# Sums of the input for the seven-product phase: formed in the normalisation phase and the ramp instead of in the attention's units

## The chip, the cores and the metric

One core of one Trainium2 chip. The metric is the device time in microseconds (us) of one execution, as the median of several runs.

## The reference

A transformer block on 2048 tokens of width 640, all in float32. Attention and a gated feed-forward network work on the same normalised input and are both added to it:

```python
xn = layernorm(x)                                # over the last axis, no weights
q, k, v = split(xn @ wqkv)                       # 32 heads of 20
mask = (i - j >= 0) & (i - j < 256)              # sliding causal window
o = softmax(where(mask, q @ k.T / sqrt(20), -1e9)) @ v
a = o @ wo
h = gelu(xn @ w_gate, approximate=True) * (xn @ w_up)     # 1728 wide
return x + a + h @ w_down
```

## The kernel before

The tokens are four chunks of 512, and the normalised input is kept transposed on chip, for each chunk as a high part `xh0` to `xh3` and a low part `xl0` to `xl3` (128 partitions, five blocks of the width, 512 tokens). Float32 products are made of three products of such parts.

**Normalisation.** For each chunk c the kernel loads and normalises four tiles of 128 tokens, transposes them on TensorE (`ln_turn`, ps_t), splits them into high and low, and makes v of the chunk before (`proj_v`, ps_v) and the first 128 columns of q and of k (`proj_qk`, ps_d). `save_qk` splits each of these into three bfloat16 parts; the last step of it is a subtraction on GpSimd (POOL, L259), and SyncE (SP, L268) then stores it to DRAM as `qd` or `kd`. POOL also makes the masks there (L467 to L473). In this part the instructions are placed by a scheduler.

**Ramp and units.** The attention is cut into 32 units: eight groups of four heads times four chunks. The order in it is written out by hand, in slots: fourteen for each unit, and ahead of unit 0 a ramp of twelve steps that are numbered -13 to -2. In the ramp `load_stack` brings q and k of the first units from DRAM into `qs` and `ks` (L494; six loads each, three for either half of the heads), and `max_pair` makes the first row maxima (ps_m on PE, L523). A unit makes the exponentials (ps_e, L582, and P on ACT, L584), POOL sets the masked corners of P to zero (`clear`, L595 and L598), and `av_unit` multiplies them with v (ps_o, L622). Between these, `pull_fill` puts in other matmuls: further columns of q, k and v, and part of the feed-forward network.

Each engine takes its instructions in the order in which they were written. SP has one queue: loads and stores alike are issued in turn, and one whose data isn't ready holds those behind it.

**The sums.** After the attention, columns of the feed-forward network are made with seven products instead of eight. That needs four sums of blocks of the input for each pair p of chunks. `x_sums(p, k, half)` forms them: ten steps s1 to s10 on POOL (L755), each a `tensor_tensor` on 128 partitions and 256 tokens, and each on the result of the one before it in its sum. Four of the steps (s3, s5, s7, s10) end a sum, which SP then stores to DRAM in `td` (L759). There are eight such calls (two pairs, two values of k, two halves), so 80 steps and 32 stores. A sum lies in one of two buffers, so a third sum waits until the first has been stored. Before, the steps are put into the units:

```python
XS0, XSN = 24, 50
for i, (p, k, half) in enumerate((p, k, half) for p in range(NC // 2) for k in range(2) for half in range(2)):
    for j, fn in enumerate(x_sums(p, k, half)):
        at(XS0 + XSN * i + 2 * j, when_free, fn)
```

`at` sets the slot, `when_free` puts the step into a waiting list, and `release(2)` takes two of that list in certain slots of a unit. `defer(n, ...)` does something n slots later, or at once where no slots run, as in the normalisation.

Of the kernel before, what the change touches and what calls it, by code (L numbers as in the profile page):

```python
# [9 lines left out]
F32 = mybir.dt.float32  # L10
# [3 lines left out]
OP = mybir.AluOpType  # L14
# [5 lines left out]
C = 512  # L20
NC = S // C
# [23 lines left out]
NQD = 9  # L45
OWN = 4, 5
WARM = 64
XS0, XSN = 24, 50
RAMP = 4.0
GAP = 16  # L50
VW = 1408
# [19 lines left out]
def block_kernel(ctx, tc, x, wqk, wv, wgu, wdo, wdl, out):  # L71
    nc = tc.nc
# [123 lines left out]
    def at(slot, fn, *a):  # L196
        acts.setdefault(slot, []).append((fn, a))
# [23 lines left out]
    def flush():  # L221
        while lates:
            fn, a = lates.pop(0)
            fn(*a)
# [4 lines left out]
    def defer(n, fn, *a):  # L229
        if now[0] is None:  # L230
            fn(*a)
        else:
            at(now[0] + n, fn, *a)

    def load_qk(t):
        raw = wrp.tile([128, KT, 128], F32, name="wr", tag="wr")
        nc.sync.dma_start(raw, wqk[t])
        return raw
# [106 lines left out]
    def first_chunk(xs, wr0, wr5, lp):  # L345
# [74 lines left out]
                save_qk(5 * i, 0, dn[i])  # L420
        return w0, w5, mv

    v0 = []
    with tc.tile_pool(name="lp", bufs=1, side="right") as lp:
        xs = [ln_load(t, lp) for t in range(2)]
        wr0 = load_qk(0)
        xs += [ln_load(t, lp) for t in range(2, 4)]
        warm = lp.tile([128, 256], BF, name="warm")[:, 0:128]
        nc.vector.memset(warm, 0.0)
        ps = psd.tile([128, C], F32, name="ps_u", tag="dn")  # L430
        for i in range(WARM):
            nc.tensor.matmul(ps[:, 0:128], warm, warm, start=True, stop=True)
        wr5 = load_qk(5)
        prep = load_v(0, v0, lp)
        next(prep)
        xs += [ln_load(t, lp) for t in range(4, 8)]
        w0, w5, mv1 = first_chunk(xs, wr0, wr5, lp)
        run(prep)
        v0 = v0[0]
        ones = lp.tile([4, 2 * C], BF, name="ones")  # L440
        nc.gpsimd.memset(ones, 0.0)
        nc.gpsimd.memset(ones[0:2], 1.0)
        for i in range(NK):
            for j in (0, 2):
                nc.sync.dma_start(ks[i][SR:64, j:j + 2].rearrange("p j t -> p (j t)"), ones)
        for c in range(1, NC):
            ln_scale(xs[4 * c:4 * c + 4], lp, mv1 if c == 1 else None)
            vs = [proj_v(v0, 4 * c - 4 + i, None if i % 2 else (psm, "mx")) for i in range(4)]
            if c == 1:
                with tc.manual_schedule(engines={mybir.EngineType.PE}):  # L450
                    lead = (cost for gen in vs for cost in gen)
                    for _ in range(VLEAD):
                        next(lead)
                    ln_turn(4 * c, xs[4 * c:4 * c + 4])
                    run(lead)
            else:
                ln_turn(4 * c, xs[4 * c:4 * c + 4])
            if c + 1 < NC:
                xs += [ln_load(t, lp) for t in range(4 * c + 4, 4 * c + 8)]
            if c == 1:  # L460
                for i in range(NQ):
                    for j in (0, 2):
                        nc.sync.dma_start(qs[i][SR + 2:64, j:j + 2].rearrange("p j t -> p (j t)"), ones[2:4])
            if c == 2:
                for z in range(4):
                    band = mask if z == 0 else lp.tile([128, D], F32, name="xi", tag="xi", bufs=8)[:, 0:288]
                    nc.gpsimd.memset(band, 0.0)  # L467
                    nc.gpsimd.affine_select(out=band, in_=band, pattern=[[1, 288]], compare_op=OP.is_ge,
                                            fill=NEG, base=32 * z - 1, channel_multiplier=-1)
                    nc.gpsimd.affine_select(out=band, in_=band, pattern=[[-1, 288]], compare_op=OP.is_ge,  # L470
                                            fill=NEG, base=256 - 32 * z, channel_multiplier=1)
                    if z:
                        nc.gpsimd.tensor_copy(mask[32 * z:32 * z + 32], band[32 * z:32 * z + 32])  # L473
                raws1 = [load_qk(1), load_qk(6)]
            if c < NC - 1:
                run(*vs)
                run(proj_qk(0, w0, c), proj_qk(5, w5, c))
            else:
                run(*[proj_v(v0, 4 * c - 4 + i) for i in range(VEARLY)])
# [261 lines left out]
            ws = nxt  # L741
        rest.append(ws)

    def x_sums(p, k, half):
        w = C // 2
        a, b = (slice((2 * p + i) * C + half * w, (2 * p + i) * C + half * w + w) for i in (0, 1))
        eh, el = xh.bitcast(F32), xl.bitcast(F32)
        live = {}

        def tile_of(i):  # L750
            live[i] = ap.tile([128, w], F32, name="tx", tag="tx")
            return live[i]

        def pool(o, i, j, op):
            nc.gpsimd.tensor_tensor(out=o, in0=i, in1=j, op=op)  # L755

        def store(i):
            t = live[i]
            defer(4, lambda: nc.sync.dma_start(td[p][i][:, k, half * w:half * w + w], t))  # L759

        def s1():
            pool(tile_of(1), eh[:, k, b], eh[:, k, a], OP.subtract)

        def s2():
            pool(live[1], live[1], el[:, k, b], OP.add)

        def s3():
            pool(live[1], live[1], el[:, k, a], OP.subtract)
            store(1)

        def s4():
            pool(tile_of(2), eh[:, k + 2, b], live[1], OP.subtract)

        def s5():
            pool(live[2], live[2], el[:, k + 2, b], OP.add)
            store(2)

        def s6():
            pool(tile_of(4), eh[:, k + 2, a], live[2], OP.subtract)

        def s7():
            pool(live[4], live[4], el[:, k + 2, a], OP.add)
            store(4)

        def s8():
            pool(tile_of(3), eh[:, k + 2, b], eh[:, k, b], OP.subtract)

        def s9():
            pool(live[3], live[3], el[:, k + 2, b], OP.add)

        def s10():
            pool(live[3], live[3], el[:, k, b], OP.subtract)
            store(3)

        return s1, s2, s3, s4, s5, s6, s7, s8, s9, s10

    NU = NG * NC
    stream = ((u, i) for u in range(NU) for i in range(8))
    fill = filler()
# [15 lines left out]
    def pull_fill(n):  # L815
        debt[0] += n
        while debt[0] > 0:
            debt[0] -= next(fill, 1.0)

    def attention():  # L820
        now[0] = -1
        load_stack(0)
        load_stack(1)
        load_stack(2)
        for i, (p, k, half) in enumerate((p, k, half) for p in range(NC // 2) for k in range(2) for half in range(2)):
            for j, fn in enumerate(x_sums(p, k, half)):
                at(XS0 + XSN * i + 2 * j, when_free, fn)
        for i in range(12):
            now[0] = i - 13
            for fn, a in tick():  # L830
                fn(*a)
            if i % 2 == 0:
                pull_max(2, now[0])
            flush()
            pull_fill(2 * RAMP)
        pull_fill(GAP / 2)
        pull_max(2, now[0])
        pull_fill(GAP / 2)
        for u in range(NU + 1):
            for i in range(NS):  # L840
                T = now[0] = NS * u + i
                for fn, a in tick():
                    fn(*a)
                if i in BURSTS:
                    pull_max(2, T)
                if i == 0 and u:
                    av_unit(u - 1)
                    flush()
                    pull_max(2, T)
                for s in SCORES.get(i, ()) if u < NU else ():  # L850
                    exp_piece(u, s)
                flush()
                if i in POOL_SLOTS or T < NS:
                    release(2)
                if u + 3 < NU and i in (KSLOT, 12):
                    load_stack(u + 3, (int(i == KSLOT),))
                pull_fill(RATE / NS)
        while acts or idle:
            now[0] += 1
            for fn, a in tick():  # L860
                fn(*a)
            flush()
            release(2)
        assert not idle
        now[0] = None
        run(fill)
        assert not acts
# [207 lines left out]
    class Job:  # L1075
# [24 lines left out]
        def store(self):  # L1100
            if self.kind == "r":
                nc.sync.dma_start(rd[self.i].rearrange("h (a t) -> (h a) t", a=4), self.t)
            elif self.kind == "t":
                nc.sync.dma_start(wtd[self.i], self.t)
            else:
                nc.sync.dma_start(self.rows, self.t)
# [417 lines left out]
```

## Time and profile before

| | us |
|---|---|
| median of 3 runs | 1049.04 |
| lowest and highest of them | 1048.1, 1049.57 |
| the profiled execution's own time | 1047.65 |
| its span in the profile | 1045.9 |

All rows of the profile are from that one execution. PE is TensorE's matmuls, PEld its weight loads, DVE VectorE, ACT ScalarE, POOL GpSimd, SPq the issues of SyncE's DMA queue. A row of a timeline has the start and the length in us, the engine, the line, the operation, what it writes and reads, and how many such instructions in a row it stands for; in brackets stands how long the engine was idle before it and what ended that. The granted clock is the share of full speed that TensorE had.

### The profile page before, as it was taken

How to read it: one execution, taken by the hardware profiler on the slowest of the kernel's cores; microseconds unless marked ns; L12 is line 12 of the kernel's file. 1: busy time of each engine (PE TensorE's matmuls, PEld its weight loads, DVE VectorE, ACT ScalarE, POOL GpSimd, SP SyncE). 2: the span in 40 equal slices, each digit the busy share in tenths (PEclk: the TensorE clock that was granted, in tenths of full speed). 3: DMA queues.
4: the chain of work that ended last, by engine and by line, in shares of the span. 5: the costliest groups of instructions: out<-in, count | busy, mean ns of one | idle time of the engine just before them, and what ended most of it. 6: DMA issues, size and time to landing. Idle time of an engine off the chain costs nothing.

```text
span 1045.9 us, 28723 instructions
## 1 busy us (share of the span) xinstructions
PE 1028.8 (98%) x10941; PEld 853.0 (82%) x10941; DVE 726.2 (69%) x2007; ACT 527.7 (50%) x1120; POOL 378.1 (36%) x543
## 2 busy tenths in 40 slices
PE   8999999999999999999999999999999999999998
PEld 7987767667788876767677888888888999999998
DVE  8845656666665565666663678877655889888887
ACT  4444667766666666656666532223324554333332
POOL 5222878876575567574745111110110000000000
PEclk9999999999999999999999999999999999999999
DMA  5641465545332354444322557676216874443342
GB/s 200 189 150 60 143 192 148 181 143 181 108 114 81 97 170 120 140 125 147 103 88 69 196 191 237 222 252 247 99 62 248 269 240 137 136 127 116 122 137 92
DMA packets 105203, 158.95 MB, mean 152 GB/s; under 512 B 15420, under 2 KB 60092, under 8 KB 105064
## 3 DMA queue, kind: packets, MB, share of 16 engines
q1 hardware_dynamic: 102680, 150.95, 45.1%
q10 hardware_dynamic: 2384, 6.16, 1.9%
q8 instruction: 86, 1.41, 0.5%
q14 instruction: 53, 0.43, 0.1%
HBM read 101.78 MB, written 54.92 MB: 150 GB/s over the span
## 4 chain that ended last, share of the span: by engine, by line
PE 87%; DVE 4%; DMA 3%; POOL 2%; SPq 1%; issue 1%; ACT 1%; DVEq 0%; POOLq 0%; ACTq 0%
PE ps_g L968 21%; PE ps L1235 21%; PE ps_d L110 20%; PE ps_e L582 7%; PE ps_v L110 7%; PE ps_o L622 5%; PE ps_m L523 4%; DVE junk L527 1%; PE ps_g L110 1%; DMA qs<-qd 1%; DMA ks<-kd 1%; PE ps_t L181 1%; SPq L494 1%; POOL pt L259 1%; PE ps_d L356 1%
## 5 line engine op out<-in xcount | busy, mean ns | idle before, releaser
L527 DVE CUSTOM_DVE_ANT_0 junk<-ps_m,mask 128x288 bf16<-128x288 f32 (+2 forms) x512 | 227.8, 445 | 143.0 <-PE ps_m L523 85.2
L584 ACT ACTIVATE P<-ps_e 128x512 f32<-128x512 f32 (+2 forms) x384 | 195.4, 573 | 59.4 <-PE ps_e L582 57.9
L1235 PE MATMUL ps<-wb,at 128*128 128x320 f32 x999 | 156.1, 309 | 0.1
L1235 PEld LDWEIGHTS ps<-wb,at 128*128 128x128 f32 x999 | 148.9, 188 | 0.5 <-issue 0.3
L595 POOL TENSOR_SCALAR_AFFINE_SELECT P<-P 128x512 f32<-128x512 f32 x128 | 84.2, 660 | 83.0 <-ACT P L584 75.4
L582 PE MATMUL ps_e<-qs,ks 124*128 124x128 bf16 (+2 forms) x704 | 107.1, 277 | 1.3 <-DVE mx L527 1.2
L110 PE MATMUL ps_d<-xh,wqh 128*128 128x512 f32 x350 | 105.2, 410 | 0.0
L110 PE MATMUL ps_d<-xh,wql 128*128 128x512 f32 x350 | 105.2, 410 | 0.0
L110 PE MATMUL ps_d<-xl,wqh 128*128 128x512 f32 x350 | 105.2, 409 | 0.0
L1235 PE MATMUL ps<-wt,at 128*128 128x320 f32 x552 | 89.3, 309 | 0.4 <-DVE u L1073 0.4
L622 PE MATMUL ps_o<-P,v 64*32 64x320 f32 (+5 forms) x2816 | 84.4, 353 | 3.0 <-DVE mx L527 1.6
L582 PEld LDWEIGHTS <-ks 124*128 124x128 bf16 x704 | 51.6, 98 | 39.7 <-issue 22.8
L1235 PEld LDWEIGHTS ps<-wt,at 128*128 128x128 f32 x552 | 82.9, 188 | 0.9 <-DVE u L1073 0.9
L1189 ACT ACTIVATE at<-ss 128x512 fp32r<-128x512 f32 x59 | 37.3, 632 | 89.6 <-DVE ss L1073 89.6
L103 POOL TENSOR_TENSOR wql<-wr,wqh 128x640 fp32r<-128x640 f32 x11 | 17.7, 1610 | 173.9 <-PE ps_g L968 129.3
L598 POOL TENSOR_SCALAR_AFFINE_SELECT P<-P 128x512 f32<-128x512 f32 x112 | 71.5, 648 | 20.6 <-ACT P L584 20.4
L622 PEld LDWEIGHTS ps_o<-P,v 64*32 64x32 f32 x2816 | 66.6, 107 | 15.0 <-DVE mx L527 6.1
L110 PEld LDWEIGHTS ps_d<-xh,wql 128*128 128x128 f32 x350 | 63.9, 189 | 13.1 <-issue 1.9
L110 PEld LDWEIGHTS ps_d<-xl,wqh 128*128 128x128 f32 x350 | 63.6, 189 | 12.2 <-issue 1.7
L110 PEld LDWEIGHTS ps_d<-xh,wqh 128*128 128x128 f32 x350 | 63.2, 189 | 12.6 <-issue 0.9
L523 PE MATMUL ps_m<-ks,qs 60*32 60x96 bf16 (+5 forms) x3008 | 64.6, 244 | 4.1 <-DVE mx L527 2.0
L259 POOL TENSOR_TENSOR pt<-r,pt 128x512 bf16<-128x512 f32 x40 | 46.8, 1170 | 54.6 <-ACT pt L258 54.5
(196 smaller groups left out, 1887.0 us busy)
## 6 DMA issues: line engine op xcount, KB each, us to landing
hr<-hd SPq DMA_DIRECT2D x104, 128.0 KB
hd<-he SPq DMA_DIRECT2D x50, 256.0 KB
wr<-wgu SPq DMA_DIRECT2D x27, 320.0 KB
qs<-qd SPq DMA_DIRECT2D x64, 120.0 KB
ks<-kd SPq DMA_DIRECT2D x64, 120.0 KB
xi<-x SPq DMA_DIRECT2D x16, 320.0 KB
qs<-qd SPq DMA_DIRECT2D x64, 80.0 KB
ks<-kd SPq DMA_DIRECT2D x64, 80.0 KB
```

The source lines that it names most:

```text
L110: nc.tensor.matmul(ps, a(k), b(k), start=n == 0, stop=n == 3 * nk - 1)
L259: nc.gpsimd.tensor_tensor(out=pt[:, l, :], in0=r, in1=pt[:, 1, :], op=OP.subtract)
L523: nc.tensor.matmul(ps[32 * h:32 * h + 32, lo:hi], q[rows, j, q0:q0 + 32], keys, start=True, stop=True, tile_position=(64 * r, 32 * h))
L527: nc.vector.tensor_tensor_reduce(out=junk[:, 0:n], in0=ps[:, 0:n], in1=mask[:, 288 - n:288], scale=1.0, scalar=NEG, op0=OP.add, op1=OP.max ...
L582: nc.tensor.matmul(ps[:, col:col + n], k[0:QROWS, j, kc:kc + 128], q[0:QROWS, j, q0:q0 + n], start=True, stop=True)
L584: nc.scalar.activation(pt[:, j, lo:hi], ps[:, lo:hi], AF.Exp, scale=SCALE)
L595: nc.gpsimd.affine_select(out=a, in_=a, pattern=[[0, 4], [1, 128]], compare_op=OP.is_ge, fill=0.0, base=0, channel_multiplier=-1)
L598: nc.gpsimd.affine_select(out=a, in_=a, pattern=[[0, 4], [-1, 128]], compare_op=OP.is_ge, fill=0.0, base=-1, channel_multiplier=1)
L622: nc.tensor.matmul(halves[h][32 * j:32 * j + 32, q0:q0 + n], v[rows, w0_:w0_ + 32], pts[u, bi][rows, j, col:col + n], start=i == 0, stop=i ...
L968: nc.tensor.matmul(ps, i, j, start=first and n == 0, stop=n == len(work) - 1, skip_group_check=True)
L1189: nc.scalar.activation(hi[:, 3:7], s, AF.Copy)
L1235: nc.tensor.matmul(ps[bank][:, 0:HD], *work[bank][j], start=bank not in begun, stop=final[p, bank] == n and j == len(work[bank]) - 1, skip ...
```

## The change

The sums of the first pair are formed in the normalisation: behind the transposes of chunk 2 those with k = 0, behind chunk 3 those with k = 1. The sums of the second pair go into the ramp, from its step -10 on, two steps a slot, and `release(2)` is called in the ramp too. The stores come one slot after their sum instead of four; in the normalisation they come at once. There the sums lie in the two buffers `he`, which the attention uses later for the feed-forward network. `x_sums` itself moves up in the file.

```diff
-XS0, XSN = 24, 50
+XS0, XSN = -10, 6
...
         def tile_of(i):
-            live[i] = ap.tile([128, w], F32, name="tx", tag="tx")
+            live[i] = (ap.tile([128, w], F32, name="tx", tag="tx") if p else
+                       hp.tile([128, C], F32, name="he", tag="he", bufs=2)[:, 0:w])
             return live[i]
...
         def store(i):
             t = live[i]
-            defer(4, lambda: nc.sync.dma_start(td[p][i][:, k, half * w:half * w + w], t))
+            defer(1, lambda: nc.sync.dma_start(td[p][i][:, k, half * w:half * w + w], t))
...
                 raws1 = [load_qk(1), load_qk(6)]
+            if c > 1:
+                for half in range(2):
+                    for fn in x_sums(0, c - 2, half):
+                        fn()
             if c < NC - 1:
                 run(*vs)
...
-        for i, (p, k, half) in enumerate((p, k, half) for p in range(NC // 2) for k in range(2) for half in range(2)):
-            for j, fn in enumerate(x_sums(p, k, half)):
-                at(XS0 + XSN * i + 2 * j, when_free, fn)
+        for i, (k, half) in enumerate((k, half) for k in range(2) for half in range(2)):
+            for j, fn in enumerate(x_sums(1, k, half)):
+                at(XS0 + XSN * i + j // 2, when_free, fn)
...
             flush()
+            release(2)
             pull_fill(2 * RAMP)
```

The steps of the sums have L435 in the changed kernel, their stores L439, the loads of `load_stack` L552, the clears L653 and L656. Two places of the order follow.

SP, before, at the loads of unit 0: the second three loads of its keys (`ks0`) stand right behind the first three, and ahead of the first store of q of chunk 2 (`qd2`). Numbers are those of the buffers.

```order
L494 DMA ks0_169<-kd0_88 40x1024
L494 DMA ks0_169<-kd0_88 20x1024
L494 DMA ks0_169<-kd0_88 60x1024
L494 DMA qs1_167<-qd1_85 40x1024
L268 DMA qd2_86<-pt_902 80x3x512
```

SP, after, the same three loads with what stands between them and the first three:

```order
L439 DMA td04_103<-he_833 128x256
L268 DMA qd2_86<-pt_938 80x3x512
L439 DMA td03_102<-he_837 128x256
L268 DMA qd2_86<-pt_938 48x3x512
L439 DMA td01_100<-he_1035 128x256
L268 DMA kd2_90<-pt_962 80x3x512
L268 DMA kd2_90<-pt_962 48x3x512
L439 DMA td02_101<-he_1040 128x256
L439 DMA td04_103<-he_1044 128x256
L552 DMA ks0_169<-kd0_88 40x1024
L552 DMA ks0_169<-kd0_88 20x1024
L552 DMA ks0_169<-kd0_88 60x1024
```

The five stores of sums here are the end of the second call of `x_sums` and most of the third; six more stand further up, among the loads of `qs0` and of the first half of `ks0`.

POOL, before, ahead of and at the clears of unit 0's P:

```order
L259 TENSOR_TENSOR pt_1392<-r_1393,pt_1392 128x512
L595 AFFINE_SELECT P_1585<-P_1585 128x4x128
L598 AFFINE_SELECT P_1585<-P_1585 128x4x128
L595 AFFINE_SELECT P_1652<-P_1652 128x4x128
L259 TENSOR_TENSOR pt_1714<-r_1715,pt_1714 128x512
L595 AFFINE_SELECT P_1707<-P_1707 128x4x128
L598 AFFINE_SELECT P_1707<-P_1707 128x4x128
```

POOL, after, the second and the third of these three pieces of P:

```order
L653 AFFINE_SELECT P_1767<-P_1767 128x4x128
L435 TENSOR_TENSOR tx_1838<-tx_1838,xl2_82 128x256
L435 TENSOR_TENSOR tx_1851<-xh3_79,tx_1838 128x256
L259 TENSOR_TENSOR pt_1843<-r_1844,pt_1843 128x512
L435 TENSOR_TENSOR tx_1851<-tx_1851,xl3_83 128x256
L435 TENSOR_TENSOR tx_1877<-xh2_78,tx_1851 128x256
L653 AFFINE_SELECT P_1833<-P_1833 128x4x128
L656 AFFINE_SELECT P_1833<-P_1833 128x4x128
```

The steps tx_1838 to tx_1877 are of the last call; all earlier calls and most of this one stand ahead of the last clears. Before, no step of a sum stands ahead of them.

More of the change, by code (lines that the diff above doesn't have):

```diff
@@ L421, in first_chunk, with x_sums, tile_of, pool @@
         return w0, w5, mv
+    def x_sums(p, k, half):
+        w = C // 2
+        a, b = (slice((2 * p + i) * C + half * w, (2 * p + i) * C + half * w + w) for i in (0, 1))
+        eh, el = xh.bitcast(F32), xl.bitcast(F32)
+        live = {}
+        def tile_of(i):
+            live[i] = (ap.tile([128, w], F32, name="tx", tag="tx") if p else
+                       hp.tile([128, C], F32, name="he", tag="he", bufs=2)[:, 0:w])
+            return live[i]
+        def pool(o, i, j, op):
+            nc.gpsimd.tensor_tensor(out=o, in0=i, in1=j, op=op)
+        def store(i):
+            t = live[i]
+            defer(1, lambda: nc.sync.dma_start(td[p][i][:, k, half * w:half * w + w], t))
+        def s1():
+            pool(tile_of(1), eh[:, k, b], eh[:, k, a], OP.subtract)
+        def s2():
+            pool(live[1], live[1], el[:, k, b], OP.add)
+        def s3():
+            pool(live[1], live[1], el[:, k, a], OP.subtract)
+            store(1)
+        def s4():
+            pool(tile_of(2), eh[:, k + 2, b], live[1], OP.subtract)
+        def s5():
+            pool(live[2], live[2], el[:, k + 2, b], OP.add)
+            store(2)
+        def s6():
+            pool(tile_of(4), eh[:, k + 2, a], live[2], OP.subtract)
+        def s7():
+            pool(live[4], live[4], el[:, k + 2, a], OP.add)
+            store(4)
+        def s8():
+            pool(tile_of(3), eh[:, k + 2, b], eh[:, k, b], OP.subtract)
+        def s9():
+            pool(live[3], live[3], el[:, k + 2, b], OP.add)
+        def s10():
+            pool(live[3], live[3], el[:, k, b], OP.subtract)
+            store(3)
+        return s1, s2, s3, s4, s5, s6, s7, s8, s9, s10
     v0 = []
@@ L742, in filler @@
         rest.append(ws)
[L744 to L750, printed above, removed]
-            live[i] = ap.tile([128, w], F32, name="tx", tag="tx")
[L752 to L795, printed above, removed]
     NU = NG * NC
```

## The prediction

> **What bounds the kernel now.** I read the engine totals first.
>
> ```profile
> span 1045.9 us, 28723 instructions
> PE 1028.8 (98%) x10941; PEld 853.0 (82%) x10941; DVE 726.2 (69%) x2007; ACT 527.7 (50%) x1120; POOL 378.1 (36%) x543
> ```
>
> TensorE (PE) has 17.1 us of idle time in the whole span. So the change can give back only PE waits, and costs whatever new PE waits it makes. The busy time by stretch says where both can be (columns: stretch, length, busy time of PE, weight load, DVE, ACT, POOL, granted clock, DMA share, GB/s).
>
> ```profile
> 46.25:106.02 59.77, 58.78 (x576) 47.72 (x574) 28.81 (x103) 25.15 (x76) 14.34 (x16) 1.00 0.37 110
> 121.00:520.00 399.00, 391.88 (x6463) 288.09 (x6448) 253.35 (x968) 258.73 (x570) 278.75 (x411) 1.00 0.46 138
> ```
>
> In the first row, the end of the normalisation and the ramp, PE idles 0.99 us and POOL works 14.34 us of 59.77. In the second, the units in which the sums run, PE idles 7.12 us and POOL works 70% of the time. Moving work from the second row to the first looks free by share. The share hides two in-order queues, POOL and SP, so I read their timelines next.
>
> ```profile
> 43.61 2.27 SPq L494 DMA_DIRECT2D qs<-qd  x6
> 45.92 3.12 SPq L494 DMA_DIRECT2D ks<-kd  x6
> 49.08 0.33 SPq L494 DMA_DIRECT2D qs<-qd  x1
> 56.05 0.82 SPq L268 DMA_DIRECT2D qd<-pt  x2
> 61.80 2.81 SPq L494 DMA_DIRECT2D ks<-kd  x6
> 64.65 2.57 SPq L494 DMA_DIRECT2D qs<-qd  x6
> 67.27 2.56 SPq L494 DMA_DIRECT2D ks<-kd  x6
> 62.48 0.38 PE L523 MATMUL ps_m<-ks,qs 60*32 60x32 bf16 x28
> SPq L268 <- POOL pt L259: 77.8, 23, 13.4
> ```
>
> SP issues the loads of unit 0 (six of qs, six of ks) by 49.04, then stands until 56.05 at a store of q that POOL has not finished: an SP store holds everything behind it (77.8 us in 23 such waits, last row). The loads are 13.4 us ahead of the first score matmul on PE at 62.48. That lead is the cover of anything put ahead of them.
>
> **The change part by part.** First what a step of the sums costs.
>
> ```profile
> L755 POOL TENSOR_TENSOR tx<-tx,xl x48: 722/736/1274, 122.3 to 516.3; 128x256 f32<-128x256 f32 x48
> 121.44 0.73 POOL L755 TENSOR_TENSOR tx<-xh,xh 128x256 f32<-128x256 f32 x1
> 122.25 1.55 POOL L755 TENSOR_TENSOR tx<-tx,xl 128x256 f32<-128x256 f32 x2
> 24.52 1.33 POOL L259 TENSOR_TENSOR pt<-r,pt 128x512 bf16<-128x512 f32 x1 [1.69 <-ACT pt L258]
> 37.69 1.16 POOL L259 TENSOR_TENSOR pt<-r,pt 128x512 bf16<-128x512 f32 x1 [11.85 <-ACT pt L258]
> 45.81 0.44 POOL L473 COPY mask<-xi 32x288 f32<-32x288 f32 x1
> 69.83 3.10 POOL L103 TENSOR_TENSOR wql<-wr,wqh 128x640 fp32r<-128x640 f32 x2
> ```
>
> A step waits for the one before it, so it starts 0.80 us after it (121.44 to 122.25). The first five steps fall into the idle 11.85 us ahead of 37.69 and cost nothing; the others start when the masks end, at 45.81 + 0.44 = 46.25.
>
> Then the stores. Sums alternate between two buffers, so s6 of each half cannot start before the store issued after s3 has landed. Two landings that POOL waited for, with their issues:
>
> ```profile
> 395.17 2.41 SPq L759 DMA_DIRECT2D td<-tx  x2
> 398.56 0.74 POOL L755 TENSOR_TENSOR tx<-xh,tx 128x256 f32<-128x256 f32 x1 [2.33 <-DMA td<-tx]
> 291.47 3.84 SPq L759 DMA_DIRECT2D td<-tx  x3
> 293.41 0.74 POOL L755 TENSOR_TENSOR tx<-xh,tx 128x256 f32<-128x256 f32 x1 [0.86 <-DMA td<-tx]
> POOL tx L755: 7.2, 5
> ```
>
> Issue to use was 3.39 us and 1.94 us; of 32 stores 5 made POOL wait (last row: the us and times that POOL waited for td). Since only late ones leave a row I take 2.4, nearer the short end. Two steps (s4, s5; 1.6 us) cover part, so each half costs POOL about 0.85 us, and 0.3 to 1.8 us with the two ends.
>
> *The first stall.* The order puts eleven stores, which need 27 steps, ahead of the second three ks loads of unit 0. Five steps are early; 22 x 0.80 = 17.6 us, two L259 between them 2.3 us (1.16 each), two store waits 1.7 us: 46.25 + 21.6 = 67.9. SP issues that store and three loads, 0.4 us each, the last at 69.1. For load to use:
>
> ```profile
> 406.17 2.97 SPq L494 DMA_DIRECT2D qs<-qd  x6
> 411.27 0.45 PE L523 MATMUL ps_m<-ks,qs 60*32 60x32 bf16 x31 [0.63 <-DMA qs<-qd]
> ```
>
> The last of these six was issued at about 408.7 and PE had it at 411.27, so 2.6 us. PE starts its first pair at 71.7, not 62.48: 9.2 us of new wait, since the 13.4 us of lead are used up.
>
> *The end of the ramp.* POOL also clears the masked parts of P, which the first ps_o needs.
>
> ```profile
> 104.97 2.49 PE L622 MATMUL ps_o<-P,v 64*32 64x320 f32 x61
> 105.38 0.64 POOL L598 TENSOR_SCALAR_AFFINE_SELECT P<-P 128x512 f32<-128x512 f32 x1
> 105.97 0.64 POOL L595 TENSOR_SCALAR_AFFINE_SELECT P<-P 128x512 f32<-128x512 f32 x1
> ```
>
> The clear of 105.38 ends at 106.02, inside PE's ps_o group: no cover. The order puts 76 steps ahead of it, 71 of them after 46.25: 71 x 0.80 = 56.8 us, beside the 14.34 us that POOL works there already. Without a single wait the clear ends at 46.25 + 56.8 + 14.34 = 117.4, 11.4 us later than before. Store waits: six halves at 0.85 = 5.1 us. The first half of the second pair pays more: its first store stands behind 18 loads (ks1, qs2, ks2: 61.80 to 69.83 above, 8.0 us) and two stores of q (0.8 us), and lands 2.4 us later, 11.2 us after the last step of the first pair; POOL has five steps, two L259 and the two wql to do meanwhile (4.0 + 2.3 + 3.1 = 9.4 us), so it waits 1.8 us. So 117.4 + 6.9 = 124.3, and PE is 18.3 us late. The first stall lies inside this and is not added.
>
> *After it.* The waits that the sums caused in the units go:
>
> ```profile
> 403.44 3.42 PE L622 MATMUL ps_o<-P,v 64*32 64x384 f32 x55 [1.61 <-DVE mx L527]
> 402.23 1.23 POOL L595 TENSOR_SCALAR_AFFINE_SELECT P<-P 128x512 f32<-128x512 f32 x2
> 465.92 1.42 PE L622 MATMUL ps_o<-P,v 64*32 64x320 f32 x48 [1.27 <-POOL P L598]
> 401.50:403.40 1.90, 0.33 (x2) 0.00 (x0) 1.06 (x3) 0.36 (x1) 1.90 (x3) 1.00 0.08 23
> 403.40:406.80 3.40, 3.37 (x68) 2.56 (x75) 1.40 (x6) 0.27 (x1) 3.32 (x6) 0.52 0.77 217
> ```
>
> The wait of 1.61 us is named after DVE, but ends with POOL's clear (402.23 + 1.23), which was late by the 2.33 us that POOL stood at a td store above. Behind it the granted clock was 0.52 for 3.40 us, so 1.63 us more. With 1.27 at 465.92 and 0.63 at 411.27 the gain is 5.1 us; at most it is all 7.12 idle plus 1.63. What is late next there is PE's own work.
>
> The long waits of the ramp bring the same half clock: those inside the ramp are covered by POOL's delay, the last adds 1.6 us. [...]
>
> The sum: 18.3 + 1.6 - 5.1 = 14.8 us. The profiled execution took 1047.65, 1.75 us around its span, and becomes 1062.4; the median of the runs, 1049.04, is 1.39 us above it, so I forecast 1063.8. Nothing else is added or removed: PE, DVE and ACT have the same instructions in the same sequence in both orders.
>
> Bounds: with no store wait at all 11.4 - 5.1 = 6.3 us, 1055. With stores at 3.4 us each half costs 1.8 us, 13 us for seven and 1 for the hold-up: 117.4 + 14 = 131.4, 25.4 us late; two half clocks 3.2, less 2 to 5 of gain: 1076. That the second pair's sums end in the ramp is not so in the order: fourteen steps stand among and behind unit 0's clears; the 76 are those ahead of the last.
>
> **The rivals.** *It gains.* If the stores did not hold the loads, and POOL had the 71 steps done in idle time, only the 5.1 us would count: 1044. For it speaks the 14.34 of 59.77. Against it, POOL's steps need 56.8 us and have 45.4 idle, and SP is in order. It decides if the ramp's 18.3 falls under 5.1. *It breaks even*, within 0.2% (2.1 us, about what a measurement of this kernel can tell from no change): the lowest ramp, 11.4, against the highest gain, 8.8, is 2.6; it would need both. *Only the first stall counts:* if the clears stood ahead of the second pair's sums, 9.2 + 1.6 - 5.1 = 5.7, 1054.7. The order speaks against it. *Steps slow beside DVE:*
>
> ```profile
> 23.70 2.50 DVE L164 TENSOR_SCALAR xi<-xi,mv,rs 128x640 f32<-128x640 f32 x3
> ```
>
> This runs beside the L259 of 24.52, which took 1.33 where the one of 37.69 took 1.16, 15% more. If all 71 steps paid that, 71 x 0.80 x 0.15 = 8.5 us would come on top, 1072. Against it speak the group's median of 736 ns, and that DVE is busy only 28.81 of the 59.77 us. [...] *Late stores:* the longer store above, from 3 us a store on: 20 us and more, 1069 to 1078. For it: SP holds a store back whenever it waits for POOL, and eight sums' stores now share the queue with the loads.
>
> **How the numbers follow.** Forecast, 1055 to 1069: 0.66. Late stores: 0.15. Slow steps: 0.05. First stall alone: 0.08. No change: 0.03. Gain: 0.03. So slower 0.94, same 0.03, faster 0.03. The range 1055 to 1076 holds the forecast, the slow steps and two thirds of the late stores, 0.8.
>
> **What would show it.** Right: PE waits some 9 us for a DMA ks<-kd at its first ps_m; its first ps_o waits for POOL's clear and starts near 123; POOL is at nine tenths from 46 to 125 and near half in the units; PE's waits at 403 and 465 are gone and stretches of half clock stand behind the ramp's waits. Wrong: the first ps_m near 62, or POOL idle for over 15 us between 46 and 125 with the clear still late, which would make the stores and not the steps the price; or PE's idle time after 130 not smaller.

## The result, and the profile after

| | before | after |
|---|---|---|
| median (lowest to highest of four runs), us | 1048.57 (1047.44 to 1049.57) | 1062.28 (1061.5 to 1064.41) |
| the profiled execution's own time, us | 1047.65 | 1064.41 |
| its span, us | 1045.9 | 1062.7 |

The ratio is 1.0134, with a 95% interval of 1.0115 to 1.0154: slower by 13.7 us by the medians. The profiled execution of after is the highest of its four, so the two profiles differ by more, 16.8 us in span.

First the engine totals of after.

```profile
span 1062.7 us, 28755 instructions
PE 1034.1 (97%) x10941; PEld 858.7 (81%) x10941; DVE 720.5 (68%) x2007; ACT 527.9 (50%) x1120; POOL 378.1 (36%) x543
```

POOL's busy time is the same to a tenth of a microsecond: the work was moved and nothing was added to it. PE is busy 5.3 us longer and idle 28.6 us instead of 17.1. The busy time by stretch shows where (columns as before: stretch, length, PE, weight load, DVE, ACT, POOL, granted clock, DMA share, GB/s).

```profile
46.00:125.00 79.00, 65.12 (x578) 52.20 (x576) 31.78 (x107) 24.98 (x77) 64.01 (x83) 0.89 0.43 132
136.00:535.00 399.00, 395.35 (x6561) 292.83 (x6560) 249.01 (x979) 263.19 (x579) 227.52 (x342) 1.00 0.44 129
66.40:76.70 10.30, 5.10 (x38) 3.96 (x39) 1.46 (x8) 0.00 (x0) 8.93 (x13) 0.50 0.47 142
100.60:107.40 6.80, 5.58 (x21) 5.59 (x22) 2.46 (x9) 1.77 (x9) 6.28 (x9) 0.50 0.75 246
127.90:131.30 3.40, 3.40 (x60) 2.59 (x45) 1.34 (x6) 1.32 (x3) 3.24 (x5) 0.50 0.38 80
```

In the ramp (first row) PE is idle 13.88 us, where it was idle 0.99 us in the row of before. In the units (second row) it is idle 3.65 us instead of 7.12, and POOL's share fell from 70% to 57%. The last three rows are the stretches of half clock: all three lie in the ramp or right behind it, and the one that stood at 403 before is gone. The timeline of PE has the waits that go with them.

```profile
71.60 0.52 PE L581 MATMUL ps_m<-ks,qs 60*32 60x32 bf16 x27 [7.97 <-DMA ks<-kd]
101.81 1.70 PE L110 MATMUL ps_v<-wvh,xh 128*128 128x320 f32 x5 [4.07 <-DVE r L273]
127.29 2.02 PE L680 MATMUL ps_o<-P,v 64*32 64x320 f32 x45 [2.42 <-POOL P L656]
149.07 0.38 PE L581 MATMUL ps_m<-ks,qs 60*32 60x32 bf16 x27 [0.53 <-issue]
```

PE's instructions are the same in the same sequence before and after, so each can be set against its like. The first ps_m was at 62.48 and is at 71.60, 9.1 us later; only one matmul of this group of 28 ran ahead of the wait, at 63.44. The ps_m of 149.07 is the one that stood here in the timeline of before:

```profile
125.62 0.38 PE L523 MATMUL ps_m<-ks,qs 60*32 60x32 bf16 x28
```

There PE is 23.45 us late. By the end of the span it is 16.8 us late, so 6.6 us were given back behind it. Why the first ps_m is late stands in SP's timeline, and the rest in POOL's timeline and in the waits:

```profile
66.72 1.94 SPq L439 DMA_DIRECT2D td<-he  x2
68.71 1.11 SPq L552 DMA_DIRECT2D ks<-kd  x3
94.58 0.73 POOL L435 TENSOR_TENSOR tx<-xh,tx 128x256 f32<-128x256 f32 x1 [4.02 <-DMA td<-tx]
126.60 0.64 POOL L656 TENSOR_SCALAR_AFFINE_SELECT P<-P 128x512 f32<-128x512 f32 x1
```

The waits (who, for whom, the total in us, the times, the longest):

```profile
DVE r L273 <- POOL pt L259: 16.4, 5, 6.5
POOL tx L435 <- DMA td<-tx: 6.0, 4, 4.0
POOL he L435 <- DMA td<-he: 5.5, 6, 2.5
```

The second three ks loads of unit 0 are issued from 68.71 to 69.82, behind a store that waited for POOL. The last clear ahead of ps_o ends at 126.60 + 0.64 = 127.24; before it ended at 106.02. POOL stood 11.5 us at stores that had not landed (last two rows). The first row of the waits is a chain that the prediction did not have: DVE makes r from the result of POOL's L259, L259 stands in POOL's order among the steps, and PE's ps_v at 101.81 waited for that r.

### The profile page after: what moved, and what is told of

The parts are those of the page before. It is cut to its first block, busy times and chain, and to the rows that moved or that the text cites. A ratio compares the mean times of both kernels' runs of the same rounds, so it can differ in the third digit from the quotient of the medians.

```text
span 1062.7 us, 28755 instructions
## 1 busy us (share of the span) xinstructions
PE 1034.1 (97%) x10941; PEld 858.7 (81%) x10941; DVE 720.5 (68%) x2007; ACT 527.9 (50%) x1120; POOL 378.1 (36%) x543
## 4 chain that ended last, share of the span: by engine, by line
PE 79%; DMA 6%; DVE 5%; POOL 5%; issue 2%; SPq 1%; ACT 1%; DVEq 0%; POOLq 0%; ACTq 0%
PE ps_g L974 20%; PE ps_d L110 18%; PE ps L1241 18%; PE ps_e L640 7%; PE ps_o L680 5%; PE ps_v L110 5%; PE ps_m L581 4%; POOL he L435 2%; DMA td<-he 2%; DVE junk L585 1%; PE ps_g L110 1%; POOL tx L435 1%; DMA hr<-hd 1%; POOL pt L259 1%; DVE at L1079 1%
## 5 line engine op out<-in xcount | busy, mean ns | idle before, releaser
L653 POOL TENSOR_SCALAR_AFFINE_SELECT P<-P 128x512 f32<-128x512 f32 x128 | 83.7, 655 | 103.0 <-ACT P L642 99.5
L656 POOL TENSOR_SCALAR_AFFINE_SELECT P<-P 128x512 f32<-128x512 f32 x112 | 71.1, 646 | 24.2 <-ACT P L642 24.2
L581 PE MATMUL ps_m<-ks,qs 60*32 60x96 bf16 (+5 forms) x3008 | 65.7, 245 | 11.5 <-DMA ks<-kd 8.0
L581 PEld LDWEIGHTS <-qs 60*32 60x32 bf16 x3008 | 34.0, 90 | 46.4 <-issue 40.9
```

Of the source, the lines that this page charges most:

```text
L581: nc.tensor.matmul(ps[32 * h:32 * h + 32, lo:hi], q[rows, j, q0:q0 + 32], keys, start=True, stop=True, tile_position=(64 * r, 32 * h))
L653: nc.gpsimd.affine_select(out=a, in_=a, pattern=[[0, 4], [1, 128]], compare_op=OP.is_ge, fill=0.0, base=0, channel_multiplier=-1)
L656: nc.gpsimd.affine_select(out=a, in_=a, pattern=[[0, 4], [-1, 128]], compare_op=OP.is_ge, fill=0.0, base=-1, channel_multiplier=1)
```

## The experiments

Each change of time is against the kernel before on the same chip: 1049.34 us (median of 17 runs) for each pair alone, for the stores from POOL's queue and for the steps three slots apart; 1049.26 us (16 runs) for the other three. A ratio, given with its 95% interval, need not be exactly the quotient of the medians.

### The first pair's sums alone

```diff
-            defer(1, lambda: nc.sync.dma_start(td[p][i][:, k, half * w:half * w + w], t))
+            defer(4, lambda: nc.sync.dma_start(td[p][i][:, k, half * w:half * w + w], t))
...
-                at(XS0 + XSN * i + j // 2, when_free, fn)
+                at(224 + 50 * i + 2 * j, when_free, fn)
```

> The sums of the first pair stay in the normalisation as in the change; those of the second pair go back into the units as before (slots 224 and later, stores four slots late). Theory (two queues: SP's stores hold the loads of unit 0, POOL's steps ahead of the clears set the end of the ramp): SP's order ahead of the second three ks0 loads is that of the changed kernel, so the first ps_m still waits some 8 us and starts near 71.7. POOL has only 35 steps after 46.25, 28 us beside the 14.34 it works there, so the clears of unit 0 are ready before PE wants them and ps_o waits for nothing. The stall of 9 us is then not inside anything: about 9.4 us, 2 us of waits for DVE's r behind it (r waits for POOL's L259), 1 to 3 us of half clock, and the waits at 403, 411 and 465 come back: 1059 to 1062. Rival (the price is the number of steps ahead of the clears alone, the first stall is slack): the clears are early, so 1048 to 1050. Rival (every late store costs by its landing): half the stores, half the price, 1055 to 1056.

Measured: 1058.66 us (1056.69 to 1061.34), ratio 1.0100 (1.0083 to 1.0117). PE's timeline, all of its waits over 1.2 us from 60 us on:

```profile
71.86 0.52 PE L581 MATMUL ps_m<-ks,qs 60*32 60x32 bf16 x27 [7.87 <-DMA ks<-kd]
414.41 3.21 PE L680 MATMUL ps_o<-P,v 64*32 64x384 f32 x59 [2.14 <-DVE mx L585]
476.53 1.42 PE L680 MATMUL ps_o<-P,v 64*32 64x320 f32 x48 [1.26 <-POOL P L656]
```

The first stall is there in full and the time is 9.3 us up by the medians, just under the 1059 to 1062 of the two-queue theory. No wait for the clears stands in the ramp: 35 steps fit into POOL's idle time there. The waits of the units are back at the same two places, so they belong to the second pair. The rival "first stall is slack" is out.

### The second pair's sums alone

```diff
-            live[i] = (ap.tile([128, w], F32, name="tx", tag="tx") if p else
-                       hp.tile([128, C], F32, name="he", tag="he", bufs=2)[:, 0:w])
+            live[i] = ap.tile([128, w], F32, name="tx", tag="tx")
...
-            defer(1, lambda: nc.sync.dma_start(td[p][i][:, k, half * w:half * w + w], t))
+            defer(1 if p else 4, lambda: nc.sync.dma_start(td[p][i][:, k, half * w:half * w + w], t))
...
-            if c > 1:
-                for half in range(2):
-                    for fn in x_sums(0, c - 2, half):
-                        fn()
...
+        for i, (k, half) in enumerate((k, half) for k in range(2) for half in range(2)):
+            for j, fn in enumerate(x_sums(0, k, half)):
+                at(24 + 50 * i + 2 * j, when_free, fn)
```

> The sums of the second pair stay in the ramp as in the change; those of the first pair go back into the units as before (slots 24 to 224). Theory: no store of a sum stands ahead of the loads of unit 0, so the first ps_m is at 62.5 as before. 36 steps of 0.80 us start only where the ramp's slots begin (some 70 us) and most stand ahead of the last clear of unit 0, which they push from 106 to about 112.5: ps_o waits some 6.5 us for POOL, 1 us more for qs0, with one half clock behind it. The waits at 403, 411 and 465 (3.5 us and 1.6 us of half clock) go, since the second pair made them. Net 4 to 6 us: 1052 to 1055. Rival (by totals: POOL idles 45.4 us between 46.25 and 106 and 28.8 us of steps fit): only the gain is left, 1043 to 1045. Rival (only the first stall counts): the same 1043 to 1045.

Measured: 1050.61 us (1048.8 to 1052.0), ratio 1.0014 (1.0003 to 1.0025). PE's timeline at the first ps_m and the first ps_o behind the clear:

```profile
62.53 0.38 PE L576 MATMUL ps_m<-ks,qs 60*32 60x32 bf16 x28
112.36 2.56 PE L675 MATMUL ps_o<-P,v 64*32 64x320 f32 x46 [4.61 <-POOL P L651]
```

The places came out as expected: the first ps_m is untouched, and ps_o is at 112.36, 6.3 us behind the end of the clear of before (106.02). PE's wait there is 4.61 us and not 6.5, since PE itself came later. The time missed: 1.3 us up by the medians, where 1052 to 1055 was expected. The two profiles are 3.1 us apart in span (1049.0 against 1045.9), still less than the 4 to 6 forecast. Part of it is the start: PE is 6.3 us late at this ps_o, where the theory had 6.5 and 1 more for qs0. Most of the step from 3.1 to 1.3 us is the choice of the run: the profiled execution of before, 1047.65 us, lies 1.7 us under the median of before here. What makes up the rest was not found. The result excludes the 1043 to 1045 of both rivals.

### The first pair's stores from POOL's queue

```diff
-            defer(1, lambda: nc.sync.dma_start(td[p][i][:, k, half * w:half * w + w], t))
+            defer(1, lambda: (nc.sync if p else nc.gpsimd).dma_start(td[p][i][:, k, half * w:half * w + w], t))
```

> As the change, but the first pair's 16 stores are issued from POOL's own queue, right behind the step that ends the sum, instead of SP's. With that the scheduler also puts more of these steps ahead of the masks. Theory: nothing of a sum stands ahead of unit 0's loads in SP's order, so the first ps_m starts at 62.5 to 66 with a wait under 4 us. Still the clears of unit 0 stand behind the same 76 steps: even if ten more of these fit into POOL's idle time ahead of 46 us (8 us), ps_o starts at 117 or later, and later by what 16 issues cost POOL (no row shows that; 0 to 1.2 us each). So the total hardly follows the first stall: 1054 to 1068. Rival (the first stall of 8 us is the price and POOL's lateness only follows from it): ps_o back to 108 to 110, total 1046 to 1052.

Measured: 1075.8 us (1073.9 to 1076.91), ratio 1.0257 (1.0239 to 1.0274). The timelines: an early wait of PE's, SP's loads of unit 0, then POOL, DVE and PE around the longest wait, and PE's wait for the clear.

```profile
50.03 1.70 PE L110 MATMUL ps_v<-wvh,xh 128*128 128x320 f32 x5 [5.31 <-DVE xl L190]
57.28 2.27 SPq L552 DMA_DIRECT2D qs<-qd  x6
59.59 4.19 SPq L552 DMA_DIRECT2D ks<-kd  x6
82.16 1.15 POOL L259 TENSOR_TENSOR pt<-r,pt 128x512 bf16<-128x512 f32 x1
83.34 0.69 DVE L273 TENSOR_TENSOR r<-ps_d,pt 128x512 f32<-128x512 f32 x1 [21.03 <-POOL pt L259]
84.09 1.70 PE L110 MATMUL ps_v<-wvh,xh 128*128 128x320 f32 x5 [15.47 <-DVE r L273]
88.39 0.52 PE L581 MATMUL ps_m<-ks,qs 60*32 60x32 bf16 x28
138.82 2.57 PE L680 MATMUL ps_o<-P,v 64*32 64x320 f32 x46 [4.72 <-POOL P L656]
```

The stores as a group (shortest, middle and longest issue in ns), and POOL's wait ahead of them:

```profile
L439 POOL DMA_DIRECT2D td<-he x16: 557/557/707, 30.7 to 84.4; - x16
```

```profile
POOL td L439 <- POOL he L435: 5.8, 16, 0.4
```

The time missed both ranges, the theory's 1054 to 1068 and the rival's. Half of the expectation held: no store of a sum stands among SP's loads any more, and the first ps_m has no wait of its own. It is not at 62.5 to 66, though, but at 88.39, because PE stands 15.47 us at the ps_v ahead of it, and 5.31 us at an earlier one. The long wait is for r, r waits for L259, and L259 stands in POOL's order behind the sums. Sixteen stores from POOL cost it 16 x 0.557 = 8.9 us and 5.8 us of waiting for their steps, 14.7 us more in the same queue. The 0 to 1.2 us for an issue had been the author's range, with no run behind it. The scheduler also moved steps ahead of the masks here, so the run changes more than who issues the stores. So the price of the first pair is not SP alone: with SP free, POOL's queue holds PE by another way. A free SP with a POOL that is no busier than in the change was not run.

### The first pair without its steps

```diff
-            nc.gpsimd.tensor_tensor(out=o, in0=i, in1=j, op=op)
+            if p:
+                nc.gpsimd.tensor_tensor(out=o, in0=i, in1=j, op=op)
...
-            defer(1, lambda: nc.sync.dma_start(td[p][i][:, k, half * w:half * w + w], t))
+            src = t if p else eh[:, k, a]
+            defer(1, lambda: nc.sync.dma_start(td[p][i][:, k, half * w:half * w + w], src))
```

> As the change, but the 40 POOL steps of the first pair are left out (so these sums are not formed); its 16 stores stay on SP and write a block of the input instead, which is there early. Theory (what holds SP is a store that waits for a step, and what delays the clears is the number of steps): the 16 stores cost SP 0.35 us each, 5.6 us before the loads of unit 0, so the first ps_m starts at 62.5 to 65. Only the second pair's steps stand ahead of the clears, as in the run with the second pair alone: ps_o waits 4.5 to 7 us for POOL near 112 to 115, and the waits at 403, 411 and 465 are gone: 1050 to 1054. Rival (the stores themselves, their number and traffic ahead of the loads, make the first stall): first ps_m still near 70, 1058 to 1062.

Measured: 1052.45 us (1051.91 to 1052.93), ratio 1.0037 (1.0022 to 1.0051). SP's sixteen stores in a row, ahead of every load of unit 0, then PE at the first two ps_m and the first ps_o behind the clear:

```profile
43.55 9.03 SPq L441 DMA_DIRECT2D td<-xh  x16
64.09 0.17 PE L583 MATMUL ps_m<-ks,qs 60*32 60x32 bf16 x1 [1.61 <-DMA ks<-kd]
65.26 0.38 PE L583 MATMUL ps_m<-ks,qs 60*32 60x32 bf16 x27 [1.00 <-DMA ks<-kd]
116.20 2.56 PE L682 MATMUL ps_o<-P,v 64*32 64x320 f32 x46 [4.68 <-POOL P L658]
```

The time lies within the theory's 1050 to 1054. The bulk of the first ps_m starts 0.3 us and ps_o 1.2 us behind the theory's ranges, far from the rival's 70. The stores cost SP 0.56 us each (9.03 / 16), not 0.35, and the scheduler put all sixteen ahead of unit 0's loads, where the change has eleven ahead of the last of them. Even so the first ps_m is only 2.8 us late; with the steps it was 9.1. So most of the first stall is stores that wait for their steps; the stores' number alone explains at most 2.8 us of it. The 40 steps and all that waited for them, the first stall among it, are worth 9.8 us of the change's time (1062.28 to 1052.45, each from its own set of runs).

### Four buffers for the second pair

```diff
-            live[i] = (ap.tile([128, w], F32, name="tx", tag="tx") if p else
+            live[i] = (ap.tile([128, w], F32, name="tx", tag="tx") if p and i in (1, 4) else
                        hp.tile([128, C], F32, name="he", tag="he", bufs=2)[:, 0:w])
```

> As the change, but the second pair's sums alternate between the two buffers tx and the two buffers he, so a step waits for a store four sums back, not two. Nothing else moves. Theory with the landing as a part of the price: POOL stood 6.0 us in 4 waits for td<-tx ahead of the clears in the changed kernel, and these go; the first stall stays (first ps_m near 71.6), the clear ends near 121 instead of 127.24, and the total falls by 5 to 6.5 us: 1055.5 to 1057.5. Rival (the number of steps alone sets the clear, the landings are covered by other work): the clear stays near 127 and the time at 1061.5 to 1063.5.

Measured: 1057.98 us (1056.93 to 1058.9), ratio 1.0089 (1.0074 to 1.0105). PE's three longest waits, and between them the ps_v that in the change stood at 101.81 behind a wait of 4.07 us:

```profile
71.97 0.52 PE L581 MATMUL ps_m<-ks,qs 60*32 60x32 bf16 x27 [7.86 <-DMA ks<-kd]
98.36 0.90 PE L110 MATMUL ps_v<-wvh,xh 128*128 128x320 f32 x5
121.03 1.42 PE L680 MATMUL ps_o<-P,v 64*32 64x320 f32 x48 [2.19 <-POOL P L656]
127.28 0.45 PE L581 MATMUL ps_m<-ks,qs 60*32 60x32 bf16 x31 [1.28 <-DVE r L273]
```

POOL's waits for stores, and the stretch around PE's wait at 121.03:

```profile
POOL he L435 <- DMA td<-he: 5.8, 6, 1.9
```

```profile
118.00:130.00 12.00, 8.53 (x142) 5.60 (x142) 6.97 (x25) 5.57 (x12) 9.66 (x16) 1.00 0.41 124
```

The waits for td<-tx (6.0 us) are gone, ps_o stands 6.3 us earlier than at 127.29, and the time is 4.3 us below that of the change; it missed the 1055.5 to 1057.5 of the theory by 0.5 us and is far from the rival's 1061.5 and more. The first stall is as it was. The wait of 4.07 us for r is gone too, so the store that POOL waited 4.02 us for had held L259, and through r also PE. Landing stores were a part of the price, as the prediction had it. How large a part follows below.

### What the sums cost in the units: two edits of the kernel before

The last two ask what the sums cost where they stood. The first puts the steps three slots apart; with that, s6 stands nine slots behind s3 instead of six.

```diff
-                at(XS0 + XSN * i + 2 * j, when_free, fn)
+                at(XS0 + XSN * i + 3 * j, when_free, fn)
```

> The kernel before with one number changed: the ten steps of a call stand three slots apart instead of two, so s6, which reuses the buffer of s3's sum, stands nine slots behind s3 instead of six while the store still comes four slots behind it. Theory (the waits in the units at 403, 411 and 465 come from POOL standing at a td store that has not landed, with the masked corners behind it): these waits go, PE's idle time after 120 falls by 3 to 5 us and the half clock behind 403 with it: 1042 to 1045. Rival (POOL's sheer load of 70% makes the clears late): nothing changes or the waits move elsewhere, 1048 to 1050.

The second issues the stores earlier and leaves the steps.

```diff
-            defer(4, lambda: nc.sync.dma_start(td[p][i][:, k, half * w:half * w + w], t))
+            defer(1, lambda: nc.sync.dma_start(td[p][i][:, k, half * w:half * w + w], t))
```

> The kernel before with only the stores' delay changed, one slot behind the sum instead of four; the steps stay two slots apart in the units. Theory (the waits at 403, 411 and 465 come from a store that is issued too late for the step that reuses its buffer): an earlier issue brings the landing earlier, the wait of 1.6 us at 403 shrinks and its half clock goes; other waits on SP stay. Gain 2.5 to 4.5 us: 1044.5 to 1047. Rival (the landing is late because the queue is full of loads just then, however early the store is issued): no change, 1048 to 1050.

Measured: three slots 1041.85 us (1041.3 to 1043.1), ratio 0.9940 (0.9926 to 0.9953); earlier stores 1045.09 us (1043.62 to 1047.35), ratio 0.9964 (0.9952 to 0.9976). Three slots came out just under the 1042 to 1045 of the theory, earlier stores within its 1044.5 to 1047. Of three slots, the totals, the units, and POOL's wait for stores:

```profile
span 1039.7 us, 28722 instructions
PE 1027.0 (99%) x10941; PEld 853.6 (82%) x10941; DVE 725.9 (70%) x2007; ACT 528.0 (51%) x1120; POOL 378.2 (36%) x543
```

```profile
121.00:520.00 399.00, 395.38 (x6558) 292.22 (x6546) 257.28 (x982) 261.21 (x575) 281.22 (x415) 1.00 0.47 139
```

```profile
POOL tx L755 <- DMA td<-tx: 0.5, 1, 0.5
```

With earlier stores, the same wait of POOL's and a wait of PE's in the units:

```profile
POOL tx L755 <- DMA td<-tx: 0.4, 1, 0.4
```

```profile
408.68 0.45 PE L523 MATMUL ps_m<-ks,qs 60*32 60x32 bf16 x31 [0.77 <-DMA qs<-qd]
```

With three slots POOL is busy 281.22 of the 399 us, as much as before (278.75), and PE's idle time there fell from 7.12 to 3.62 us, the same as the change brought (3.65). So the waits at 403 and 465 came from a buffer that was taken again too soon, not from POOL's load: both edits remove them. The wait at 411 is another: with earlier stores PE still stands 0.77 us at the same matmul (now at 408.68) for a load of qs, though POOL no longer waits for stores there. It is gone with three slots and in the change; what in SP's queue makes that load late was not taken apart. The version with three slots is faster than both kernels: by the medians 7.5 us under the kernel before and some 20 us under the change.

## Why the prediction was right, point by point

The sign and the two mechanisms held. The size came out closer (1062.28 against 1063.8) than its terms deserve, and that is partly luck: the terms below miss by up to 4.6 us and in part cancel, and the profiled execution took 1064.41 us where 1062.4 was forecast for it.

*The price of a step.* 0.80 us start to start held for nearly all steps. The commonest kind of step in the ramp of after, with the shortest, middle and longest duration in ns:

```profile
L435 POOL TENSOR_TENSOR tx<-tx,xl x24: 722/732/747, 83.4 to 130.1; 128x256 f32<-128x256 f32 x24
```

Two steps were slow, the first two behind the masks, and they ran beside DVE's L164:

```profile
46.46 2.61 DVE L164 TENSOR_SCALAR xi<-xi,mv,rs 128x640 f32<-128x640 f32 x4
47.58 1.15 POOL L435 TENSOR_TENSOR he<-xh,he 128x256 f32<-128x256 f32 x1 [1.36 <-DMA td<-he]
48.80 0.86 POOL L435 TENSOR_TENSOR he<-he,xl 128x256 f32<-128x256 f32 x1
```

The rival "steps slow beside DVE" is out as a price: the two lost some 0.55 us against 0.73 each, where 8.5 us were feared for all 71. The effect itself is there: the step that ran wholly beside L164 (46.46 to 49.07) took 1.15 us, the next, beside it for its first 0.27 us, 0.86, and the third, behind it, 0.73. Which DVE work it takes is not shown here.

*The first stall.* Forecast: the last load issued at 69.1 and ps_m at 71.7. Measured: the last of the three issues ends at 69.82 and so starts near 69.45, and ps_m is at 71.60. That the end agrees to 0.1 us is luck in part: the load came some 0.4 us later, and PE had it 2.15 us after its issue, not 2.6. The runs with the first pair alone and without its steps show the cause of the stall.

*The end of the ramp.* Forecast: the clear ends at 124.3. Measured: 127.24. Two terms were off against each other. The store waits were put at 6.9 us and were 11.5. The largest was the hold-up behind the 18 loads, put at 1.8 and measured at 4.02: the store was issued at 90.25, as counted, but was usable only at 94.58, 4.3 us later instead of the 2.4 taken from the units.

```profile
90.25 1.25 SPq L439 DMA_DIRECT2D td<-tx  x2
```

Without its store waits the clear would have ended at 127.24 - 11.5 = 115.7, not 117.4; that base was 1.7 us too high, probably because it counts a step's 0.07 us behind the one before it also where L259 stands between the two. So of the 21.2 us by which this clear is late (127.24 against 106.02), 11.5 are waits for stores and 9.7 come from the steps, where 6.9 and 11.4 had been forecast: the mechanism was right, and the term for the stores was too small.

*Nine tenths.* POOL was to be at nine tenths from 46 to 125. It was at 64.01 of 79, eight tenths, and idle 14.99 us, which is just at the 15 us that the prediction had named as a sign that stores and not steps are the price. By the balance above they share it about evenly. The runs settle only a part: the waits for td<-tx were worth 4.3 us of the time, and 40 steps together with their store waits and most of the first stall 9.8. No run took away the steps alone, or the 5.5 us of waits for td<-he alone.

*The first stall lies inside the end of the ramp.* This held for the sum, but the working passed over how. POOL's L259 feeds DVE's r, and r frees what ps_v writes; that gave the 4.07 us wait at 101.81 and the 15.47 us with POOL's own stores. PE came to ps_o already so late that only 2.42 us of wait were left there. Alone, the two parts of the change cost 9.3 and 1.3 us; together 13.7, some 3 us more than their sum.

*After the ramp.* Forecast: 5.1 us back. Measured: 3.47 us less idle time (7.12 to 3.65) and the half clock at 403 gone (0.52 for 3.40 us, an estimated 1.6 us): 5.1. Set against each other, the matmuls of 149.07 and of the end give 6.6 us; where the other 1.5 us lie was not taken apart.

*The half clock.* The last wait of the ramp was to add 1.6 us. The stretch from 127.90 to 131.30 is PE at full work (3.40 of 3.40 us busy) and half clock (0.50), an estimated 1.7 us more from these two. That the earlier stretches are covered held as well, since PE met a wait behind each of them.

The two deviations partly cancel: PE 23.45 us late behind the ramp where 18.3 + 1.6 = 19.9 was forecast, and 1.5 us more given back. Of the rivals, *it gains* and *it breaks even* are out by the interval; *only the first stall counts* (1054.7) is out, since ps_o does wait for the clear and the second pair alone makes the clear 6.3 us late. *Late stores* is partly true: stores held POOL 11.5 us, 4.6 more than forecast, but not the 20 us and more of the rival, and the time stayed under its 1069.

## What to carry to other kernels

An engine with idle time is not free time: what counts is who stands behind the moved steps in its order, and in the order of each queue that takes their results. List those for the engine, for its DMA queue and for whatever another engine's buffer waits for, and price the first of each that another engine needs. Before moving work away from where it causes waits, look at why it waits: here a buffer was reused six slots after its sum, and nine slots removed the waits that the move was paying for.

## What the runs showed of the hardware

How long PE waits does not alone decide whether the clock is halved behind it. In before, a wait of 1.61 us was followed by 3.40 us at 0.52; with four buffers a wait of 2.19 us at 121.03 was followed by full clock (1.00 from 118 to 130). The three stretches of half clock of after (0.50), about 10.3, 6.8 and 3.4 us, are near three, two and one times 3.4 us. No run here shows what sets that length, or why the clock fell behind the one wait and not behind the other. A store that was issued behind 18 loads took 4.3 us to be usable, where the two in the units had taken 1.9 and 3.4.
